# Moving two operands of TensorE to other places modulo 256 in SBUF

## The chip, the cores and the metric

The kernel runs on one core of one Trainium2 chip. The metric is the device time of one execution in microseconds. Before the change, three runs took 605.35, 607.12 and 607.37 us; their median is 607.12. One further execution was profiled.

## What the reference computes

Attention in which each query sees the keys of a narrow window and a summary of every block of 32 keys (the maximum of the keys, the mean of the values), and then a feed-forward layer with a squared ReLU:

```python
# q, k, v: (4, 8, 768, 64); block 32, window 16
k_sum = k.reshape(B, H, nb, block, D).max(axis=3)
v_sum = v.reshape(B, H, nb, block, D).mean(axis=3)
scores_l = scale * np.matmul(q, k.transpose(0, 1, 3, 2))     # kept where |i - j| < window
scores_s = scale * np.einsum('bhsd,bhnd->bhsn', q, k_sum) + np.log(block)
a = softmax(concatenate([scores_l masked, scores_s]))
x = np.matmul(a, concatenate([v, v_sum]))                     # -> (3072, 512)
h = x @ w_in                                                  # w_in (512, 2048)
g = s * np.maximum(h, 0.0) ** 2 + b
out = g @ w_out                                               # w_out (2048, 512)
```

## The kernel before, in words

The 3072 tokens are worked off in 12 chunks `c` of 256. The order of all work is written out by hand in one long string of step names (`FIRST_ORDER`, `REST_ORDER`); each engine takes its own instructions in that order, and all transfers are issued from SyncE's queue. Each operand of the large matrix products is split in two float32r parts, an upper one (`xh`, `wh`, `gh`) and a lower one (`xl`, `wl`, `gl`), and a product is three matmuls: lower by upper, upper by lower, upper by upper.

For a chunk, the steps are:
- scores `S` (L307), masks and exponentials, turned blocks on VectorE (L388), values `V` (L439); these give the attended rows `xh` and `xl`.
- the hidden layer `H` (L507): for each of 16 slices `f` of 128 hidden units, 12 matmuls of 256 columns into `ph`. The moving operand is `xh` or `xl`, the stationary one (loaded into the array ahead of the matmul) a slice of `wl` or `wh`. Two slices, 24 matmuls, share one bank `ph`.
- for each pair `q` of slices: ScalarE takes ReLU and square out of `ph` into a tile `g`, GpSimd applies `s` and `b` and forms sums of g's parts (L573 to L582), ScalarE rounds them into the upper half of a tile `gs` (L589), VectorE subtracts that for the lower half (L593).
- the output layer. Chunks 0 to 3 do it as `P` (L552), 6 matmuls of 512 columns a slice. Chunks 4 to 11 do it as `p` (`project_seven`, L672): for each `q`, seven products of sums instead of eight, 21 matmuls of 256 columns into four banks `acc`. The stationary operand is a part of `gs`. The moving one is a weight (`wh`, `wl`, 12 matmuls) or a sum of weights (9 matmuls), which is streamed from HBM into the tile `ring`.

In the steady part the order on TensorE is H of two slices (24 matmuls), p of one `q` (21), and so on; once a chunk, H of four slices (48), the values and scores of the next chunks, and p of two `q` (42) follow each other. In chunk 11 and the end of chunk 10 no scores are left to do.

The sums of weights are made once, in the tile `spare` (the same place as `ring`, earlier in time), and stored in HBM as `combos`. For chunks 4 to 11, `load_combo` (L612) loads three parts of 128 x 512 float32 for each `q` into one half of `ring`. The last two `q` of chunk 11 use tiles `late` instead: four lie in the places of the values (`vw`), two in a place of `qk`.

Places in SBUF come from the pools in the order in which they are opened; within a pool, tiles follow each other, each padded to 32 bytes. In bytes of a partition, the program before has these places:

| tile | pool | start | start modulo 256 |
|---|---|---|---|
| `wh` (and other slots) | slots | 4352 + 8192 n | 0 |
| `wl` | wring | 69888 + 4096 n | 0 |
| `ring`, `spare` | arena | 135424 | 0 |
| `kraw`, `vraw`, `o` | stage | 147712, 151808 | 0 |
| `ksum`, `rs` | small | 155904 and on | several |
| `gs` (both halves) | acts | 157120, 164288 | 192 |
| `r`, `g` | acts | 171456, 175552 | 192 |
| `xh`, `xl`, `pT` and others | p2 | 179648 and on | 192 for the large ones |
| `qk` | p3 | 207360, 213280 | 0, 32 |
| `vw` (and four `late`) | p3 | 219200 + 2048 n | 64 |

The parts of these tiles that TensorE reads start at multiples of 512 bytes (stationary) or 1024 bytes (moving) behind the tile's start, so modulo 256 they lie where the tile lies. The lower half of `gs` starts 3584 = 14 x 256 bytes behind the upper.

Of the kernel before, what the change touches and what calls it, by code (L numbers as in the profile page):

```python
# [9 lines left out]
F32 = mybir.dt.float32  # L10
# [7 lines left out]
P = 128  # L18
# [26 lines left out]
def windowed_attention_then_relu2_ffn(ctx, tc, qk, vwin, kt, vt, kq, vrow, wp, out):  # L45
# [4 lines left out]
    const = ctx.enter_context(tc.tile_pool(name="const", bufs=1))  # L50
    slots = ctx.enter_context(tc.tile_pool(name="slots", bufs=NF // 2))
    wring = ctx.enter_context(tc.tile_pool(name="wring", bufs=NF))
    arena = ctx.enter_context(tc.tile_pool(name="arena", bufs=1))
    stage = ctx.enter_context(tc.tile_pool(name="stage", bufs=2))
    kept = ctx.enter_context(tc.tile_pool(name="kept", bufs=1, space=bass.MemoryType.DRAM))
    small = ctx.enter_context(tc.tile_pool(name="small", bufs=2))
    acts = ctx.enter_context(tc.tile_pool(name="acts", bufs=2))
    p2 = ctx.enter_context(tc.tile_pool(name="p2", bufs=2))
    p3 = ctx.enter_context(tc.tile_pool(name="p3", bufs=3))
    ps_po = ctx.enter_context(tc.tile_pool(name="ps_po", bufs=2, space=bass.MemoryType.PSUM))  # L60
# [918 lines left out]
```

## Time and profile before

| | |
|---|---|
| median of three runs | 607.12 us |
| the profiled execution | 605.87 us |
| its span, first to last instruction | 603.9 us |
| granted TensorE clock, mean | 0.995 |
| TensorE busy | 584.5 us (97%) |
| VectorE busy | 438.2 us (73%) |
| ScalarE busy | 349.0 us (58%) |
| GpSimd busy | 299.5 us (50%) |
| DMA traffic | 127.34 MB, 211 GB/s on average |

A share of busy time is an average over stages. In views that group instructions a row has the line in the kernel, the engine and operation, what is written and read, how often it ran, the busy time in us and the mean length of one in ns. A matmul's length includes its way through the array, so matmuls overlap: the pace is read from the starts, or from the length of a whole piece divided by its count. The chain of work that ended last is followed back from the last instruction; in order of time it lists pieces with their start and length. PE is TensorE's matmul, PEld its loading of the stationary operand, DVE VectorE, ACT ScalarE, POOL GpSimd, SP SyncE.

### The profile page before, as it was taken

To read this page: it belongs to the slowest core of one execution; us is meant where nothing else is said; L and a number is where in the kernel's file an instruction comes from. 1 tells how busy PE (TensorE), PEld (TensorE's weight loads), DVE (VectorE), ACT (ScalarE), POOL (GpSimd) and SP (SyncE) were. 2 spreads that over 40 slices of the span, in tenths; PEclk is the share of its full clock that TensorE was granted. 3 is DMA by queue.
4 is the path that set the end of the run, shared out by engine and by line. 5 is a ranking of instruction groups with operands and counts; after the bars stand their busy time and mean duration, and the time that the engine had idled before them with its cause. 6 is when DMAs were issued, how large, how long until landed. Compare 5 with 4: busy or idle time off the path is not lost.

```text
span 603.9 us, 15345 instructions
## 1 busy us (share of the span) xinstructions
PE 584.5 (97%) x5816; PEld 555.0 (92%) x5816; DVE 438.2 (73%) x1033; ACT 349.0 (58%) x808; POOL 299.5 (50%) x499
## 2 busy tenths in 40 slices
PE   6999999999999998889999999999999999999996
PEld 5798898889899897889999999999999999999996
DVE  6999988799698699675698689587588488322323
ACT  5999899275596662733563564563563563433432
POOL 5320012590584563356645655655745755635643
PEclk9999999999999999899999999999999999999999
DMA  8999633064634974877776886765766756564540
GB/s 349 384 394 381 240 116 114 1 210 124 223 108 145 345 234 147 277 245 241 249 240 195 256 257 186 257 188 196 242 181 197 239 180 186 173 221 150 178 149 35
DMA packets 65401, 127.34 MB, mean 211 GB/s; under 512 B 7408, under 2 KB 17648, under 8 KB 65328
## 3 DMA queue, kind: packets, MB, share of 16 engines
q1 hardware_dynamic: 65328, 126.38, 62.9%
q8 instruction: 45, 0.74, 0.5%
q14 instruction: 28, 0.23, 0.1%
HBM read 111.52 MB, written 14.68 MB: 209 GB/s over the span
## 4 chain that ended last, share of the span: by engine, by line
PE 70%; DVE 12%; ACT 7%; DMA 6%; issue 2%; SPq 1%; POOL 1%; DVEq 0%; ACTq 0%; POOLq 0%
PE ph L507 33%; PE acc L672 24%; PE po L552 6%; DVE pT L388 4%; PE pav L439 3%; PE ps L307 2%; DMA qk<-in_qk_dram 2%; DMA ring<-combos 2%; DVE gs L539 1%; ACT wraw L124 1%; ACT wraw L123 1%; DVE qk L330 1%; DVE vhalf L173 1%; DMA wraw<-in_wp_dram 1%; DVE spare L642 1%
## 5 line engine op out<-in xcount | busy, mean ns | idle before, releaser
L593 DVE TENSOR_TENSOR gs<-g,gs 128x896 fp32r<-128x896 f32 x64 | 70.8, 1106 | 102.0 <-ACT gs L589 101.3
L565 ACT ACTIVATE g<-ph 128x512 f32<-128x512 f32 x64 | 38.3, 598 | 161.4 <-PE ph L507 138.7
L573 POOL TENSOR_SCALAR g<-g,sb_col 128x512 f32<-128x512 f32 x64 | 64.2, 1003 | 132.7 <-ACT g L569 116.6
L388 DVE STREAM_TRANSPOSE pT<-qk 32x256 f32<-32x256 f32 x288 | 125.6, 436 | 4.8
L672 PE MATMUL acc<-wh,gs 128*128 128x256 f32 x512 | 121.2, 280 | 0.2 <-DVE gs L593 0.2
L507 PE MATMUL ph<-xh,wl 128*128 128x256 f32 x760 | 120.0, 280 | 0.4 <-DVE wl L145 0.4
L507 PE MATMUL ph<-xh,wh 128*128 128x256 f32 x760 | 118.7, 278 | 0.0
L507 PE MATMUL ph<-xl,wh 128*128 128x256 f32 x760 | 118.6, 278 | 0.0
L507 PEld LDWEIGHTS ph<-xh,wl 128*128 128x128 f32 x760 | 103.9, 189 | 4.6 <-ACT r L521 1.2
L507 PEld LDWEIGHTS ph<-xl,wh 128*128 128x128 f32 x760 | 101.7, 188 | 0.0
L507 PEld LDWEIGHTS ph<-xh,wh 128*128 128x128 f32 x760 | 101.4, 188 | 0.0
L672 PE MATMUL acc<-ring,gs 128*128 128x256 f32 x558 | 95.2, 279 | 3.4 <-DMA ring<-combos 3.4
L672 PEld LDWEIGHTS acc<-wh,gs 128*128 128x128 f32 x512 | 91.6, 188 | 1.5 <-issue 0.8
L672 PEld LDWEIGHTS acc<-ring,gs 128*128 128x128 f32 x558 | 78.1, 188 | 4.0 <-DMA ring<-combos 4.0
L552 PE MATMUL po<-wh,gs 128*128 128x512 f32 x224 | 76.7, 394 | 0.0
L672 PE MATMUL acc<-wl,gs 128*128 128x256 f32 x256 | 71.2, 278 | 0.0
L589 ACT CAST gs<-g 128x896 fp32r<-128x896 f32 x64 | 59.9, 936 | 17.3 <-PE acc L672 9.3
L269 POOL COPY vw<-vsum 24x256 f32<-24x256 f32 x88 | 40.9, 498 | 46.1 <-DMA vw<-in_vwin_dram 19.6
L349 ACT ACTIVATE qk<-qk,mn 128x120 f32<-128x120 f32 x144 | 55.1, 384 | 5.6 <-DVE mn L330 4.9
L552 PE MATMUL po<-wl,gs 128*128 128x512 f32 x128 | 50.2, 392 | 0.0
L552 PEld LDWEIGHTS po<-wh,gs 128*128 128x128 f32 x224 | 42.1, 188 | 8.4 <-DVE mn L330 0.2
L578 POOL TENSOR_TENSOR g<-g 128x256 f32<-128x256 f32 x64 | 47.0, 734 | 4.6
(134 smaller groups left out, 918.4 us busy)
## 6 DMA issues: line engine op xcount, KB each, us to landing
ring<-combos SPq DMA_DIRECT2D x186, 256.0 KB
wraw<-in_wp_dram SPq DMA_DIRECT2D x32, 512.0 KB
qk<-in_qk_dram SPq DMA_DIRECT2D x44, 369.0 KB
vw<-in_vwin_dram SPq DMA_DIRECT2D x48, 256.0 KB
combos<-spare SPq DMA_DIRECT2D x16, 512.0 KB
out_dram<-o SPq DMA_DIRECT2D x24, 256.0 KB
kraw<-in_kt_dram SPq DMA_DIRECT2D x12, 384.0 KB
vraw<-in_vt_dram SPq DMA_DIRECT2D x12, 252.0 KB
```

The lines of the kernel that those rows point to most:

```text
L269: nc.gpsimd.tensor_copy(vw_t[c, p][WIN:KR, e], vsum[bi][WIN : WIN + NB, 2 * p + e, :].unsqueeze(1).to_broadcast([NB, NSUB, D]),)
L349: nc.scalar.activation(pr, pr, AF.Exp, bias=mn_of[c, p][:, n : n + 1], scale=-1.0, accum_out=sums_of(c, p)[:, n : n + 1])
L388: nc.vector.transpose(to[BLOCK * k : BLOCK * (k + 1), :, rows], src)
L439: nc.tensor.matmul(oi, vw[:KR, e, i, :], pi[:KR], start=True, stop=True)
L507: nc.tensor.matmul(ph, w[:, kc * P : (kc + 1) * P], x[:, kc], start=(n == 0), stop=(n == len(terms) - 1))
L552: nc.tensor.matmul(po[c, t], a[:, t * P : (t + 1) * P], w[:, 512:], start=(f == 0 and n == 0), stop=(f == NF - 1 and n == len(terms) - 1),)
L565: nc.scalar.activation(gg[c, q][:, : 2 * T], ph_of.pop((c, q)), AF.Relu)
L573: nc.gpsimd.tensor_scalar(g, g, s_col, b_col, ALU.mult, ALU.add)
L578: nc.gpsimd.tensor_tensor(g[:, 4:6], g[:, 0:1].to_broadcast([P, 2, P]), g[:, 1:3], ALU.subtract)
L589: nc.scalar.copy(halves[c, q][0], gg[c, q][:, P:])
L593: nc.vector.tensor_tensor(gl, gg.pop((c, q))[:, P:], gh.bitcast(F32), ALU.subtract)
L672: nc.tensor.matmul(to, g[:, k], w, start=(q == 0 and side == 0 and m == 0), stop=(q == NF // 2 - 1 and m == 2 and side == (bank != "m")),)
```

## The change

Three pools are opened, each with one tile that nothing writes or reads: 64 bytes a partition ahead of `arena`, 128 bytes ahead of `acts` and 64 bytes ahead of `p2`.

```diff
     wring = ctx.enter_context(tc.tile_pool(name="wring", bufs=NF))
+    ctx.enter_context(tc.tile_pool(name="gap_arena", bufs=1)).tile([P, 16], F32, name="gap_arena")
     arena = ctx.enter_context(tc.tile_pool(name="arena", bufs=1))
     stage = ctx.enter_context(tc.tile_pool(name="stage", bufs=2))
     kept = ctx.enter_context(tc.tile_pool(name="kept", bufs=1, space=bass.MemoryType.DRAM))
     small = ctx.enter_context(tc.tile_pool(name="small", bufs=2))
+    ctx.enter_context(tc.tile_pool(name="gap_acts", bufs=1)).tile([P, 32], F32, name="gap_acts")
     acts = ctx.enter_context(tc.tile_pool(name="acts", bufs=2))
+    ctx.enter_context(tc.tile_pool(name="gap_p2", bufs=1)).tile([P, 16], F32, name="gap_p2")
     p2 = ctx.enter_context(tc.tile_pool(name="p2", bufs=2))
```

By the order of the pools, what lies behind the first gap starts 64 bytes later: `ring` and `spare` at 64 modulo 256, and with them `stage` and `small`, also by 64. What lies behind the second starts 192 bytes later: `gs`, `r` and `g` at 128 modulo 256. Behind the third, all is 256 bytes later, so `p2` and `p3` keep their places modulo 256. The order of the instructions, their shapes, their waits and the transfers are the same.

## The prediction

> **What bounds the kernel now.** I began with the page of the profiled execution: busy shares, then the chain that ended last.
>
> ```profile
> span 603.9 us, 15345 instructions
> PE 584.5 (97%) x5816; PEld 555.0 (92%) x5816; DVE 438.2 (73%) x1033; ACT 349.0 (58%) x808; POOL 299.5 (50%) x499
> ...
> PE ph L507 33%; PE acc L672 24%; PE po L552 6%; DVE pT L388 4%; PE pav L439 3%; PE ps L307 2%; DMA qk<-in_qk_dram 2%; DMA ring<-combos 2%; DVE gs L539 1%; ACT wraw L124 1%; ACT wraw L123 1%; DVE qk L330 1%; DVE vhalf L173 1%; DMA wraw<-in_wp_dram 1%; DVE spare L642 1%
> ```
>
> TensorE is busy 97% of the span, and the chain lies on its matmuls of L507 (the hidden layer, H) and L672 (the seven products, p). So what the change is worth is decided by the pace of these matmuls, and by whether any operand comes late. The next view is the chain in order of time, in one chunk of the steady part; the columns are start, length in us, and what.
>
> ```profile
> 395.31 2.83 PE ph L507 x24
> 398.14 2.47 PE acc L672 x21
> 400.61 2.73 PE ph L507 x24
> 403.35 2.38 PE acc L672 x21
> 405.73 2.83 PE ph L507 x24
> ...
> 416.15 2.83 PE ph L507 x24
> ...
> 424.18 2.38 PE acc L672 x21
> 426.57 5.65 PE ph L507 x48
> 432.22 2.01 PE pav L439 x64
> ...
> 436.04 5.02 PE acc L672 x41
> ```
>
> The chain has no holes. But TensorE has two paces for the same work. 24 matmuls of H take 2.73 or 2.83 us, which is 113.8 or 117.9 ns each; 21 of p take 2.38 or 2.47, 113.3 or 117.6 ns. The paces alternate: slow H, slow p, quick H, quick p, slow H. So a pace survives the step from H to p, and changes at the step from p to H. A matmul at the slow pace costs 4.1 to 4.3 ns more; I use 4.2.
>
> Which data are read does not explain it. In H the moving operand is x (192 modulo 256) and the stationary one a weight (0); in p the moving one is a weight or the ring (0) and the stationary one a half of g (192). Both paces occur with both. The last two chunks show that the product's number does not explain it either:
>
> ```profile
> 525.97 5.14 PE acc L672 x42
> 531.11 2.73 PE ph L507 x24
> ...
> 562.37 5.46 PE ph L507 x48
> 567.83 4.76 PE acc L672 x42
> 572.59 2.83 PE ph L507 x24
> ```
>
> The 42 products that start a chunk are slow at 525.97 (122 ns each, their restart included) and quick at 567.83 (113.3), on the same buffers; at 531.11 the same step from p to H made H quick, where the one behind 436.04 is followed by a slow H in the other chunks. So the pace has a memory, and a step from p to H usually tips it.
>
> **The change, part by part.** It adds three empty tiles of 64, 128 and 64 bytes a partition. No instruction, wait, queue entry or byte of traffic is added, so the fixed part of the sum is 0. What moves, by the order of the pools: the ring tile (and `spare`, the same place earlier) from 0 to 64; behind it also `stage` and `small`, by 64; all of `acts`, g and its halves alike, from 192 to 128; `p2` by 256, so its places modulo 256 stay, and `p3` likewise. Five things could cost.
>
> (1) The landing of the ring, 186 loads of 2048 bytes a partition. The trace has loads of the same packet size to both kinds of place: values go to 64 modulo 256 (390.5 to 391.5, where values alone are under way), ring parts to 0 (575.0 to 576.0, ring alone). From the DMA view of both windows:
>
> ```profile
> DMA packets 192, 0.36 MB, mean 361 GB/s; under 512 B 23, under 2 KB 23, under 8 KB 191
> ...
> q1 hardware_dynamic: 191, 0.34, 89.5%
> ...
> DMA packets 160, 0.28 MB, mean 279 GB/s; under 512 B 24, under 2 KB 24, under 8 KB 160
> ...
> q1 hardware_dynamic: 160, 0.28, 72.7%
> ```
>
> Values: 0.895 x 16 engines x 1.0 us = 14.3 us over 168 large packets (191 less 23 small ones), 85 ns; ring: 0.727 x 16 = 11.6 us over 136, 86 ns. So nothing, with 2 ns as a generous bound (the small packets are counted into both). A ring load is 8 packets on each of 16 engines, so 16 ns late at most, on loads for which TensorE waited 3.4 us three times in all (quoted below). I take 0; bound 0 to 0.05 us.
>
> [...]
>
> (2) VectorE, ScalarE and GpSimd on g and its halves, all now at 128 where all were at 192, so their offsets to one another stay.
>
> ```profile
> L593 DVE TENSOR_TENSOR gs<-g,gs 128x896 fp32r<-128x896 f32 x64 | 70.8, 1106 | 102.0 <-ACT gs L589 101.3
> L573 POOL TENSOR_SCALAR g<-g,sb_col 128x512 f32<-128x512 f32 x64 | 64.2, 1003 | 132.7 <-ACT g L569 116.6
> ...
> L349 ACT ACTIVATE qk<-qk,mn 128x120 f32<-128x120 f32 x144 | 55.1, 384 | 5.6 <-DVE mn L330 4.9
> ...
> L349 ACT ACTIVATE spare<-spare,mn 128x120 f32<-128x120 f32 x32 | 12.3, 388 | 0.1
> ...
> PE acc L672 <- DMA ring<-combos: 3.4, 3, 2.4
> ...
> PE acc L672 <- DVE gs L593: 0.2, 1, 0.2
> ```
>
> The same exponential at two differently placed tiles takes 384 and 388 ns: 1% either way is the bound, 11 ns on the 1106. VectorE stands idle 102 us ahead of this subtraction, and TensorE waited 0.2 us for its result in the whole run. If that cover were gone, 64 x 11 ns = 0.7 us would show, as later p groups. I take 0.
>
> (3) `stage` and `small`, 64 further: the row loads, the output rows and their stores. Priced as (1) and (2), off TensorE's path but for the last store: 0.
>
> (4) TensorE's reading inside p. Moving and stationary operand now lie 64 apart (weights 0 against halves 192). Afterwards the ring against the halves is 64 to 128, again 64 apart, but weights against halves is 0 to 128: apart by 128. The trace has that distance in one place only: `late`, at 64 in the four `vw` places, against halves at 192. The `late` parts at 0 follow it.
>
> ```profile
> L672 PE MATMUL acc<-ring,gs 128*128 128x256 f32 x558 | 95.2, 279 | 3.4 <-DMA ring<-combos 3.4
> L672 PE MATMUL acc<-late,gs 128*128 128x256 f32 x18 | 3.1, 281 | 0.0
> ...
> 594.66 0.52 PE L672 MATMUL acc<-late,gs 128*128 128x256 f32 x3
> 595.01 0.28 PE L672 MATMUL acc<-wh,gs 128*128 128x256 f32 x1
> ...
> 597.14 0.52 PE L672 MATMUL acc<-late,gs 128*128 128x256 f32 x3
> 597.50 0.28 PE L672 MATMUL acc<-wh,gs 128*128 128x256 f32 x1
> ```
>
> From three `late` matmuls at 64 to the next matmul it is 0.35 us, from three at 0 it is 0.36: no difference at this resolution. The mean lengths, 281 against 279 ns, bound it at 2 ns. It would meet 12 of the 21 matmuls of each p, 768 in eight chunks, and 384 of 512 columns in the four chunks before (L552), where the halves also stand against weights: 1152 x 2 ns = 2.3 us. I take 0.2 us, near the timeline's nothing. No row excludes a gain; rival B prices that.
>
> (5) TensorE's reading at the steps between H and p. Now operands of neighbouring matmuls coincide modulo 256 there: from H to p, x and the halves both at 192; from p to H, ring and weight both at 0. Afterwards both pairs stand 64 apart, as inside H today. The steps from p to H are where the pace tips, so this part touches the seat of the two paces. I cost it at 0 for the forecast because the two chunk starts above show different outcomes on the same places: something other than the place carries the pace, and the instruction order, which the change leaves alone, is the nearest candidate. Its bounds are the rivals.
>
> [...]
>
> Sum: 0 + 0 + 0 + 0.2 + 0 = 0.2 us on the execution's own 605.87 us (603.9 of span, 2.0 around it), 606.1. The median of the runs, 607.12, is 1.25 above that execution; I forecast on its scale, 607.3 us.
>
> **The rivals.** A chunk of 360 matmuls has, by the rows above, 3 x 45 + 48 + 42 = 225 slow and 135 quick ones. Sums of L672 (512 + 558 + 256 + 18 = 1344, 168 a chunk) make eight chunks.
>
> B, *the tipping ends on the quick side* (faster). If coinciding places are what throws the pace from quick to slow, taking them away keeps a quick pace quick. All quick: 8 x 225 x 4.2 ns = 7.6 us less, 599.5. More likely some restarts still begin slow, as at 525.97: about half, 603.5. For it: the tipping sits at exactly the steps whose distance changes, and in the middle chunks H behind L552 (weight against weight, again 0 on 0) also begins slow:
>
> ```profile
> 180.16 0.64 PE L507 MATMUL ph<-xh,wl 128*128 128x256 f32 x4
> 180.64 0.62 PE L507 MATMUL ph<-xl,wh 128*128 128x256 f32 x4
> 181.09 0.62 PE L507 MATMUL ph<-xh,wh 128*128 128x256 f32 x4
> ```
>
> The first four take 0.48 us, the next four 0.45. Against it: from H to p operands coincide as well, and nothing tips.
>
> C, *the pace sticks on the slow side* (slower). The same steps also throw slow back to quick, four times a chunk. Each chunk's products start slow behind the values and scores (436.04). If no step tips, that pace lasts the whole chunk. Price: 8 x 135 x 4.2 ns = 4.5 us, 611.8 with the forecast's 0.2. It decides where a chunk's first H behind the double group is slow and the next one is slow too; up to two quick pairs left a chunk it is still 2 us, slower. Against it: what L552 does, where H recovers by itself in the fifth matmul.
>
> D, *the change does not do what it says*: the places do not come out as listed, or no reader feels them; 607.1.
>
> **How the numbers follow.** Forecast 0.40, B 0.32, C 0.24, D 0.04. A measurement of this kernel tells about 0.3% (1.8 us) from no change; its own three runs lie 2.0 us apart. So faster is B's share, same is the forecast and D less what falls out of the band, slower is C and that rest: 0.32, 0.42, 0.26. The forecast's own range is 605.5 to 609.5 (run scatter, and 2.3 us of part 4). Into B the range goes to 602.0, past its half, leaving out about 0.13; into C to 611.5, just short of all slow, leaving out 0.06.
>
> **What would show it.** In the chain in order of time, the pieces of 24 and 21 must keep alternating between 2.83/2.47 and 2.73/2.38: then part 5 is right. All pieces at 2.73/2.38 show B, all at 2.83/2.47 C. The mean length of L672 on `wh` against `ring` shows part 4; waits of TensorE for `ring` and `gs` over 4 us would break parts 1 and 2. A third pace, below 113 or above 118 ns, in p alone would make the prediction wrong in a way that no rival prices.

## The result, and the profile after

The changed kernel took 610.45 us, the median of 9 runs (608.84 to 614.23), where the kernel before took 607.12 in the same comparison (605.35 to 608.1). The two medians lie 3.3 us apart. The ratio on record is 1.0083, with a 95% interval from 1.0063 to 1.0104, which would be 3.8 to 6.3 us; it is not the quotient of the two medians, which is 1.0055. By either figure the kernel is slower, and all nine runs after lie above all nine before. The forecast was no change, 607.3.

The page of the profiled execution after, which took 612.74 us: busy shares and three of the costliest groups (busy us, mean ns of one, idle time before them).

```profile
span 611.0 us, 15345 instructions
PE 593.2 (97%) x5816; PEld 563.3 (92%) x5816; DVE 438.3 (72%) x1033; ACT 349.4 (57%) x808; POOL 300.3 (49%) x499
...
L675 PE MATMUL acc<-wh,gs 128*128 128x256 f32 x512 | 123.9, 285 | 0.2 <-DVE gs L596 0.2
...
L675 PE MATMUL acc<-ring,gs 128*128 128x256 f32 x558 | 96.8, 282 | 4.0 <-DMA ring<-combos 4.0
...
L596 DVE TENSOR_TENSOR gs<-g,gs 128x896 fp32r<-128x896 f32 x64 | 71.2, 1113 | 109.1 <-ACT gs L592 108.5
```

and, of the kernel before, the row on `wh`:

```profile
L672 PE MATMUL acc<-wh,gs 128*128 128x256 f32 x512 | 121.2, 280 | 0.2 <-DVE gs L593 0.2
```

The instructions are the same 15345; the lines stand three further down (H is L510, p is L675). TensorE is busy 8.7 us longer, and the other engines hardly: VectorE 438.3 against 438.2 us, its subtraction 1113 ns against 1106. The products grew by 3 ns on the ring (279 to 282) and 5 ns on `wh` (280 to 285).

The same kernel's waits of TensorE (in all, times, longest):

```profile
PE acc L675 <- DMA ring<-combos: 4.0, 3, 2.4
...
PE acc L675 <- DVE gs L596: 0.2, 1, 0.2
```

They were 3.4 and 0.2 us. The 0.6 us more on the ring belong to the first products of chunk 4: TensorE reached them 0.79 us sooner than before (247.47 us against 248.26) and waited there for the same loads. So no wait explains the loss. What did change is seen in the chain in order of time (start, us, what):

```profile
260.99 2.59 PE acc L675 x15
263.59 3.77 PE ph L510 x24
...
393.74 5.13 PE acc L675 x42
398.87 2.83 PE ph L510 x24
401.70 2.50 PE acc L675 x21
404.20 2.83 PE ph L510 x24
...
430.83 5.65 PE ph L510 x48
...
440.30 5.13 PE acc L675 x42
```

and, for the length of a chunk, two rows of the same view of the kernel before:

```profile
390.17 5.14 PE acc L672 x42
...
436.04 5.14 PE acc L672 x42
```

The alternation of 2.83/2.47 and 2.73/2.38 is gone. From chunk 5 on every 24 matmuls of H take 2.83 us (117.9 ns each) and every 21 of p 2.50 (119.0 on average). From one double group (p of two `q`, 42 matmuls) to the next it is 46.56 us (440.30 - 393.74) where it was 45.87 (436.04 - 390.17): 0.69 us a chunk. The pieces say where it comes from: three H of a chunk go from 2.73 to 2.83 (0.30), three p from 2.38 to 2.50 (0.36), three p from 2.47 to 2.50 (0.09), together 0.75 by rounded lengths.

That this is pace, with no waiting and no clock in it, shows in the windows over the same four chunks (stretch, length, TensorE busy and matmuls recorded, granted clock, DMA share, GB/s); of the kernel before:

```profile
298.44:481.90 183.46, 183.46 (x1953) 1.00 0.70 221
```

and of the kernel after, with one stretch of chunk 4 ahead of it:

```profile
262.00:266.00 4.00, 4.00 (x23) 0.57 0.85 242
...
300.62:486.86 186.24, 186.24 (x1953) 1.00 0.69 218
```

TensorE is busy without a gap in both, at a granted clock of 1.00, and the four chunks take 2.78 us more. The 7.1 us between the two spans thus split up: 2.18 up to the first of these double groups (298.44 and 300.62), 2.78 in these four chunks, 1.62 in the next two, 0.52 at the end. Of the first 2.18, 1.5 us comes with a lower granted clock around 262 us (0.57 over these 4 us, where the kernel before had 1.00): 15 products took 2.59 us where the same 15 took 2.03 before, and 24 of H 3.77 where the later ones take 2.83. That is no part of the change: the run e3 below, whose pace is that of before, takes 2.82 and 3.54 us for the same two pieces. So 5.6 us of the 7.1 is the change in this pair of executions, more than the 3.3 us between the medians and inside the interval of the ratio.

### The profile page after: what moved, and what is told of

Read it like the earlier page. It is cut to its first block, busy times and chain, and to the rows that moved or that the text cites. A ratio compares the mean times of both kernels' runs of the same rounds, so it can differ in the third digit from the quotient of the medians.

```text
span 611.0 us, 15345 instructions
## 1 busy us (share of the span) xinstructions
PE 593.2 (97%) x5816; PEld 563.3 (92%) x5816; DVE 438.3 (72%) x1033; ACT 349.4 (57%) x808; POOL 300.3 (49%) x499
## 4 chain that ended last, share of the span: by engine, by line
PE 65%; DVE 14%; ACT 8%; DMA 6%; issue 3%; SPq 2%; POOL 1%; DVEq 0%; ACTq 0%; POOLq 0%
PE ph L510 31%; PE acc L675 25%; DVE pT L391 5%; PE po L555 4%; PE pav L442 3%; DMA ring<-combos 2%; PE ps L310 2%; DMA vraw<-in_vt_dram 2%; DVE gs L542 1%; ACT wraw L126 1%; DVE spare L645 1%; ACT wraw L127 1%; DVE vhalf L176 1%; ACT pr L352 1%; DMA qk<-in_qk_dram 1%
## 5 line engine op out<-in xcount | busy, mean ns | idle before, releaser
L596 DVE TENSOR_TENSOR gs<-g,gs 128x896 fp32r<-128x896 f32 x64 | 71.2, 1113 | 109.1 <-ACT gs L592 108.5
L675 PE MATMUL acc<-wh,gs 128*128 128x256 f32 x512 | 123.9, 285 | 0.2 <-DVE gs L596 0.2
L510 PE MATMUL ph<-xh,wl 128*128 128x256 f32 x760 | 120.9, 281 | 0.1
L510 PE MATMUL ph<-xl,wh 128*128 128x256 f32 x760 | 120.2, 281 | 0.0
L510 PE MATMUL ph<-xh,wh 128*128 128x256 f32 x760 | 120.1, 280 | 0.0
L510 PEld LDWEIGHTS ph<-xh,wl 128*128 128x128 f32 x760 | 105.2, 190 | 4.0 <-DVE wl L148 0.8
L510 PEld LDWEIGHTS ph<-xh,wh 128*128 128x128 f32 x760 | 102.7, 189 | 0.0
L510 PEld LDWEIGHTS ph<-xl,wh 128*128 128x128 f32 x760 | 102.7, 189 | 0.0
L675 PE MATMUL acc<-ring,gs 128*128 128x256 f32 x558 | 96.8, 282 | 4.0 <-DMA ring<-combos 4.0
L675 PEld LDWEIGHTS acc<-wh,gs 128*128 128x128 f32 x512 | 92.4, 189 | 1.4 <-issue 0.8
L675 PEld LDWEIGHTS acc<-ring,gs 128*128 128x128 f32 x558 | 79.5, 189 | 4.8 <-DMA ring<-combos 4.6
L675 PE MATMUL acc<-wl,gs 128*128 128x256 f32 x256 | 72.1, 282 | 0.0
```

The source lines that it names most:

```text
L510: nc.tensor.matmul(ph, w[:, kc * P : (kc + 1) * P], x[:, kc], start=(n == 0), stop=(n == len(terms) - 1))
L596: nc.vector.tensor_tensor(gl, gg.pop((c, q))[:, P:], gh.bitcast(F32), ALU.subtract)
L675: nc.tensor.matmul(to, g[:, k], w, start=(q == 0 and side == 0 and m == 0), stop=(q == NF // 2 - 1 and m == 2 and side == (bank != "m")),)
```

## The experiments

The two paces of TensorE are called quick (113.3 to 113.8 ns a matmul of 256 columns) and slow (117.6 to 118). My theory after the result was that the places of the operands relative to one another, modulo 256, decide at the step from p to H whether the pace tips, and that this is one effect of ring and halves together. The rivals were that one moved operand alone is read more slowly where it now lies, that the absolute place counts, and that one of the other tiles moved along (`stage`, `small`) does it.

This table has all runs; each ratio goes against runs of the kernel before in the same comparison (medians of 605.25 to 607.12 us), and the chunk is read, as above, between the double groups around 390 and 436 us.

| kernel | ring / halves | H | p | chunk, us | us | ratio (95%) |
|---|---|---|---|---|---|---|
| before | 0 / 192 | alternates | alternates | 45.87 | 607.12 | |
| after | 64 / 128 | all slow | all slow, 119.0 | 46.56 | 610.45 | 1.0083 (1.0063 to 1.0104) |
| e1_ring_only | 64 / 192 | all quick | 116.2 | 45.46 | 602.53 | 0.9941 (0.9916 to 0.9966) |
| e2_halves_only | 0 / 128 | slow behind the double group, then quick | 119.0 | 45.98 | 606.82 | 1.0010 (0.9984 to 1.0036) |
| e3_others_only | 0 / 192 | as before | as before | 45.87 | 606.61 | 1.0011 (0.9987 to 1.0035) |
| e4_halves_at_64 | 0 / 64 | quick but for one piece | slow | 45.70 | 604.61 | 0.9973 (0.9951 to 0.9996) |
| e5_ring_128 | 128 / 192 | all slow | all slow | 46.41 | 611.09 | 1.0087 (1.0055 to 1.0119) |
| e6_ring_128_halves_64 | 128 / 64 | all quick | 118.1 | 45.65 | 604.60 | 0.9976 (0.9951 to 1.0001) |
| e7_lower_weights_128 | 0 / 192, `wl` at 128 | quick, 114.8 | slow, 118.1 | 45.84 | 605.79 | 1.0005 (0.9981 to 1.0030) |
| e8_all_by_64 | 64 / 0, weights 64, x 0 | as before | as before | 45.86 | 605.32 | 1.0006 (0.9973 to 1.0040) |
| e9_one_tip | 128 / 192 | one quick a chunk, else slow | 116.2 once, else slow | 46.30 | 609.81 | 1.0067 (1.0043 to 1.0091) |
| e10_last_part_64 | 0, 0, 64 / 192 | alternates or all slow | alternates or all slow | 45.66; 46.46 when slow | 607.40 | 1.0029 (1.0010 to 1.0048) |
| e11_last_part_back | 64, 64, 0 / 128 | all quick | slow | 45.70 | 604.30 | 0.9983 (0.9961 to 1.0005) |
| e12_last_part_192 | 0, 0, 192 / 192 | alternates | alternates | 45.76 | 606.13 | 1.0012 (0.9981 to 1.0043) |

In all of them the weights lie at 0 and x at 192 unless the table says otherwise, and every kernel issues the same instructions; only e9 issues two groups of them in another order. The edits are empty tiles in pools of their own, in this form, with 16 (64 bytes), 32 or 48 floats:

```diff
+    ctx.enter_context(tc.tile_pool(name="gap_arena", bufs=1)).tile([P, 16], F32, name="gap_arena")
```

### The three parts of the change, each alone

**e1_ring_only**: the ring at 64, all else as before.

```diff
+ gap of 64 bytes ahead of arena, gap of 192 bytes ahead of stage
```

> Only the ring is moved to 64 modulo 256; stage, small, g, its halves and all behind keep their places modulo 256. Theory T1 (the step from p to H tips the pace because the last moving operand, the ring, and the weight loaded meanwhile lie at the same place modulo 256): that coincidence is gone, so the pace sticks on the slow side as in the changed kernel, pieces of 24 at 2.83 us throughout, about 611 us. Theory T2 (weights and halves 128 apart inside p are what slows): weights against halves are 64 apart as before, so the alternation of 2.83 and 2.73 stays, 607 to 608 us.

It took 602.53 us, 0.9941 of the kernel before. The chain in order of time:

```profile
387.76 5.15 PE acc L674 x42
...
423.96 5.45 PE ph L509 x48
...
433.22 5.15 PE acc L674 x42
438.37 2.73 PE ph L509 x24
441.10 2.44 PE acc L674 x21
```

Every H is quick, the one behind the double group too, and p takes 2.44 us, between 2.38 and 2.47. A chunk is 45.46 us. So the first half of the change, by itself, is a gain: rival B of the prediction, which was priced at 603.5 with half of the slow pieces made quick. T1 and T2 both missed it. The timeline of one p shows why its 2.44 us lie between the two paces:

```profile
400.65 0.28 PE L674 MATMUL acc<-wh,gs 128*128 128x256 f32 x1
...
401.33 0.51 PE L674 MATMUL acc<-ring,gs 128*128 128x256 f32 x3
...
403.10 0.62 PE L509 MATMUL ph<-xh,wl 128*128 128x256 f32 x4
```

The six matmuls ahead of the ring take 0.68 us (113 ns each), the fifteen from there on 1.77 (118). So this p starts quick and is slow from its first matmuls on the ring, which now lie 128 from the halves: the pace can turn inside a group too.

**e2_halves_only**: g and its halves at 128, all else as before.

```diff
+ gap of 192 bytes ahead of acts, gap of 64 bytes ahead of p2
```

> Only g and its halves are moved, to 128 modulo 256; the ring stays at 0, the rest keeps its places modulo 256. T1: ring and weight still coincide at the step from p to H, so the pace goes on tipping, pieces of 24 alternate, 607 to 608 us, and p itself may run at a third pace near 119 ns. T2: weights against halves are 128 apart, all pieces slow, about 611 us. A third possibility is that the step from H to p (x and halves, both at 192 before, now 64 apart) is needed for the tipping: then all slow as well, with p at 2.50.

It took 606.82 us, ratio 1.0010. Its chain:

```profile
397.21 2.82 PE ph L509 x24
400.04 2.50 PE acc L674 x21
402.53 2.74 PE ph L509 x24
...
438.01 5.18 PE acc L674 x42
443.19 2.82 PE ph L509 x24
```

Here only the H behind the double group is slow, and the others are quick, a gain; p takes 2.50 us throughout, as in the changed kernel, a loss; the two nearly cancel. The time and p's pace are those that T1 expected, the pieces of H are not: the alternation is gone although ring and weight still coincide. Neither part alone slows the kernel. A sum of the two, -0.6% and +0.1%, would be -0.5%; together they give +0.8%. So the loss is not that either operand is simply read more slowly at its new place.

**e3_others_only**: `stage` and `small` 64 further on, ring, g and halves where they were modulo 256 (256 bytes further on).

```diff
+ gap of 64 bytes ahead of stage, gap of 192 bytes ahead of acts
```

> Only stage and small are moved by 64; ring, halves, x and weights keep their places modulo 256 (all behind stage stands 256 bytes further on). T1 and T2: nothing that TensorE reads in H or p changes modulo 256, so the time stays at 607 us with the alternation of 2.83 and 2.73. If stage and small, or places beyond 256 bytes, were the cause, it would be 610 us or more.

It took 606.61 us, ratio 1.0011, and its pieces alternate as before, with the same 45.87 us a chunk. So `stage` and `small` do not cause the loss, and 256 bytes more for halves and x change nothing.

### Other distances

**e4_halves_at_64**: halves at 64, ring at 0. **e5_ring_128**: ring at 128, halves at 192. **e6_ring_128_halves_64**: both. **e7_lower_weights_128**: the lower weights `wl` at 128, all else as before. **e8_all_by_64**: everything that TensorE reads in H and p 64 further on, so that each distance is that of before.

```diff
  e4
+ gap of 128 bytes ahead of acts, gap of 128 bytes ahead of p2
  e5
+ gap of 128 bytes ahead of arena, gap of 128 bytes ahead of stage
  e6
+ gap of 128 bytes ahead of each of arena, stage, acts and p2
  e7
+ gap of 128 bytes ahead of wring, gap of 128 bytes ahead of arena
  e8
+ gap of 64 bytes ahead of slots
```

> g and its halves at 64 modulo 256, ring at 0: weights and ring against halves are 64 apart the other way round (the halves ahead), x against halves 128 apart, ring against weight coincide. T1: the step from p to H still tips, alternation, 607 us. T2: weights and halves are 64 apart, so no slowing by 128, alternation, 607 us. If the step from H to p needs its coincidence, all slow at 611 us, or all quick near 600 us if that step is what throws the pace to slow.

e4 took 604.61 us, ratio 0.9973: from chunk 5 on H is quick (2.74 us for 24) but for the first piece behind the double group of chunk 10 (531.62, 2.83), and p slow (2.47 for 21). None of the expectations has this pattern.

> Only the ring is moved, to 128 modulo 256; halves and x stay at 192, weights at 0. Theory T3 (what counts is the distance modulo 256 between the matmul's moving operand and the stationary operand loaded meanwhile: 64 or 192 inside a group allows two lasting paces, quick 113.3 ns and slow 117.8 ns; 128 inside a group forces a slow one near 119 ns; the distance at the step between groups decides which one follows): inside p all distances are 64 or 192 again, so p can be quick where it was slow with the ring at 64. The step from p to H is now 128. If that step leaves the pace alone, and H enters quick, all is quick: pieces of 24 at 2.73 and of 21 at 2.38, about 599 us. If it tips as a distance of 0 does, the alternation stays, 606 us. A theory that only the ring at exactly 64 is good gives 606 us or more.

e5 took 611.09 us, ratio 1.0087, as slow as the changed kernel, with the halves where they were. Its chain:

```profile
393.35 5.14 PE acc L674 x42
398.49 2.83 PE ph L509 x24
401.32 2.47 PE acc L674 x21
403.79 2.83 PE ph L509 x24
...
439.76 5.14 PE acc L674 x42
```

All slow, at 46.41 us a chunk. So the loss of the changed kernel is not tied to its own places: another pair gives it too. T3 expected 599 or 606 us and missed.

> Ring at 128, g and halves at 64, x at 192, weights at 0. T3: inside p the distances are 192 (weights) and 64 (ring), so two paces are possible; from H to p the distance is 128, which threw p to slow in the run with halves alone at 64, so H quick at 2.73 and p slow at 2.47, 603 to 605 us. If the ring at 128 keeps p quick, 599 to 601 us.

e6 took 604.60 us, ratio 0.9976. The ring at 128, which made e5 slow in every piece, is here beside halves at 64, and H is all quick (2.73), as T3 expected: again it is the pair that counts.

> Only the lower weights (wl) are moved, to 128 modulo 256; ring at 0, halves and x at 192, upper weights at 0. T3: H begins with wl as its stationary operand, so the step from p to H is 128 instead of 0, inside H and p all distances stay 64 or 192. If a distance of 0 at that step is what tips, the tipping ends although the ring has not moved: one pace throughout, all quick 599 us or all slow 611 us. If the tipping stays, the coincidence at this step is not its cause, 606 us.

e7 took 605.79 us, ratio 1.0005: H almost quick (2.75 or 2.76 us), p slow (2.48). Moving a third operand also breaks the alternation, but H and p do not get one pace throughout, which T3 expected where the tipping ends.

> Everything from the upper weights on is moved by 64, so all distances between weights, ring, halves and x stay as before while every place modulo 256 changes. T3 (distances alone count): same alternation of 2.83 and 2.73, same 606 us. A theory of absolute places (64 is bad for the ring, 128 for the halves) gives another pattern or time.

e8 took 605.32 us, ratio 1.0006. Its chain:

```profile
394.89 2.83 PE ph L508 x24
397.71 2.47 PE acc L673 x21
400.19 2.73 PE ph L508 x24
402.92 2.38 PE acc L673 x21
```

This is the kernel before, piece by piece. All four kinds of operands have moved by 64 modulo 256 and nothing has changed. So the absolute place does not count, as far as this one shift shows (45.86 us a chunk against 45.87); the distances do.

### Where the pace is handed over

**e9_one_tip**: e5, with the last two products of `q` = 1 exchanged in chunks 4 to 10, so that the double group ends on a weight (0) and not on the ring (128), once a chunk. All places stay those of e5.

```diff
  e5, and in do():
+        if name[0] == "p" and name[1:].split(".")[1:] in (["1", "5"], ["1", "6"]) and name[1:].split(".")[0] != "11":
+            name = name[:-1] + {"5": "6", "6": "5"}[name[-1]]
```

> Ring at 128 as in the run where every piece was slow, and for q = 1 of chunks 4 to 10 the last two of the seven products change places, so that this p ends on a weight (at 0, the weight loaded meanwhile at 0): the step that tips in the kernel before, now once a chunk, right behind the slow double group. Places are the same as in that all-slow run but for nothing. T3 with memory (the step from a ring at 128 leaves the pace as it is, quick or slow): from the first H behind the double group on all is quick, 24 at 2.73 and 21 at 2.38, until the next scores, about 600 us. If a ring at 128 makes slow of itself, H or p turns slow again at the first p that ends on the ring, 608 to 611 us.

It took 609.81 us, ratio 1.0067. Its chain:

```profile
436.08 5.14 PE acc L674 x42
441.22 2.74 PE ph L509 x24
443.96 2.44 PE acc L674 x21
446.40 2.83 PE ph L509 x24
```

In chunks 5 to 10 the H right behind the exchanged products is quick, at the one place of the chunk that was touched; only the first six matmuls of the p behind it are quick (0.68 us), and from its products on the ring on all is slow. That is the second of the two expectations; the 600 us of T3 were missed. In chunk 4, where the products had just waited for the ring, the H behind them stays slow (2.83 at 261.23). So what p ends on has a hand in the pace of H, though not alone. Other engines' reads and writes lie where they lie in e5, so this speaks for TensorE's own operands. It is worth 0.11 us a chunk (46.41 to 46.30), too little for the two ratios to tell apart.

**e11_last_part_back**: the changed kernel, with only the last third of each half of the ring, which the last product reads, put back to 0 modulo 256.

```diff
  the changed kernel, and
-            held["ring"] = arena.tile([P, 3072], F32R, name="ring", tag="ring")
+            held["ring"] = arena.tile([P, 3200], F32R, name="ring", tag="ring")
-        k = 512 * (3 * (q % 2) + n)
+        k = 1600 * (q % 2) + 512 * n + 48 * (n == 2)
```

> The changed kernel, with only the third of the ring that the last product of each p reads taken back to 0 modulo 256; the other two thirds stay at 64, g and its halves at 128. T3 (the last product and its step alone hand the pace to H): the last moving operand and the weights coincide again and are 128 from the halves, as with the halves alone moved, so H turns quick, 24 at 2.73 behind nearly every p, while p stays slow near 2.50: 606 to 608 us. If H is slow in the changed kernel because of what p as a whole is, H stays at 2.83 and the time at 610 us.

It took 604.30 us, ratio 0.9983 to the kernel before. Its chain:

```profile
388.19 5.15 PE acc L675 x42
...
424.62 5.46 PE ph L510 x48
...
433.89 5.15 PE acc L675 x42
439.04 2.74 PE ph L510 x24
441.77 2.48 PE acc L675 x21
```

Every H is quick (24 in 2.74, 48 in 5.46 us), as T3 expected, and a chunk takes 45.70 us where the changed kernel took 46.56; the time is lower than the 606 to 608 us that were expected. Three of the 21 matmuls of a p read from another place, and the 24 of H behind them change their pace. This is the strongest reading of the study: the loss in H sits at the last product of p and the step from it to H.

**e10_last_part_64** and **e12_last_part_192**: the kernel before, with the last third of each half of the ring at 64 or at 192.

```diff
  e10 and e12, the tile as in e11; e10:
+        k = 1600 * (q % 2) + 512 * n + 16 * (n == 2)
  e12:
+        k = 1600 * (q % 2) + 512 * n + 48 * (n == 2)
```

> The kernel before, with only the third of the ring that the last product of each p reads moved by 64 (places 64 modulo 256); weights, the other two thirds, halves and x as before. T3: 18 of 21 products are 64 from the halves as before and can be quick, the last three are 128 away; the step from p to H is then the one that made H quick each time in the run with the whole ring at 64. So 24 at 2.73 throughout, 21 near 2.40, about 599 us, faster than both kernels. If the three products at 128 bring back a slow p, 602 to 603 us as there; if the tipping has another seat, the alternation, 606 us.

e10 took 607.40 us, ratio 1.0029. In e1 a last product at 64 went with an H that was always quick; here it does not. Its chain, in chunks 5, 7 and 10:

```profile
303.48 2.83 PE ph L507 x24
306.31 2.48 PE acc L672 x21
308.79 2.83 PE ph L507 x24
...
395.59 2.73 PE ph L507 x24
398.32 2.39 PE acc L672 x21
400.71 2.83 PE ph L507 x24
...
530.75 2.83 PE ph L507 x24
```

The same program, on the same places, runs chunks 5 and 10 all slow and chunks 6 to 9 alternating. So the last product's place is not the whole of it: the earlier products of p, or the pace that was there before, count too. The slow chunks use up what the others gain: chunks 5 to 10 take 269.92 us (298.33 to 568.25) where the kernel before took 269.39 (298.44 to 567.83). The medians lie 1.8 us apart (607.40 against 605.63); whether other executions have more slow chunks, the one profiled cannot show. The 599 us of T3 were missed.

> The kernel before, with only the third of the ring that the last product of each p reads moved to 192 modulo 256, where the halves lie too (distance 0 in the last three matmuls, 192 at the step to H). So far a p that was quick until its last product has always been followed by a slow H (distances 64, 128 or 192 there), and a slow p was followed by a quick or a slow one. If the distance at the step decides alone, 192 keeps the pace inside H and would leave a quick p followed by a quick H: all quick, 599 us, or all slow, 611 us. If a quick p is followed by a slow H whatever the place, H and p alternate as before, 605 to 608 us.

e12 took 606.13 us, ratio 1.0012, alternating as before with the order turned: in chunks 5 to 9 the H behind the double group is quick (2.72) and the next slow (2.83). That is the last of the three expectations: a quick p is again followed by a slow H. No layout tried beats e1.

## Why the prediction was wrong

The measured 610.45 us lies beyond the forecast's own 605.5 to 609.5, and inside the wider range only because that was stretched toward rival C.

**Steps (1), (2) and (3), at 0, were right.** A packet of 2048 bytes took 84 ns before and after (median, 570 to 590 us, where most land in the ring), TensorE waited 4.0 us for the ring and 0.2 for the halves, VectorE's subtraction stayed within the 1% bound (1113 against 1106 ns), and e3 shows 1.0011 for `stage` and `small`.

**Step (4), p with weights and halves 128 apart, was too small.** I took 0.2 us from a timeline of six matmuls. A slow p of 21 went from 2.47 to 2.50 us, which over 6 pieces in each of 8 chunks is 1.4 us, inside the bound of 2.3. It is the third pace above 118 ns that the prediction named as a sign that no rival prices. The 128 alone does not make it: e11 has the same distance between weights and halves, and its p takes 2.47 or 2.48. In the first four chunks, where the halves also stand 128 from the weights, twelve matmuls of 512 columns went from 2.75 us (169.20 to 171.95 in the timeline of before) to 2.78 (169.19 to 171.97), some 2.5 ns each, 0.9 us over 352 of them. It does not show in the time: the first products of chunk 4 began at 247.47 us where they had begun at 248.26, and waited there for the ring as before.

**Step (5), the steps between H and p, at 0, failed, and with it the sign.** I had put the seat of the paces at the step from p to H, which e9 and e11 bear out for the pace of H, and then priced the change of that very step at nothing, "because the two chunk starts above show different outcomes on the same places: something other than the place carries the pace, and the instruction order, which the change leaves alone, is the nearest candidate". The inference was wrong. Two outcomes on the same places show that the place alone doesn't determine the pace; they don't show that it has no part in it. With one and the same order of instructions, the runs have H alternating (before), all quick (e1, e6, e11) and all slow (after, e5). Together with the third pace of p, what stood at 0 is 5.6 us in the traces.

**Rival C is what happened**, but for the third pace of p: no step tips any more, and the pace sticks on the slow side, from the H behind the double group on (398.87, then 404.20), as C's condition had it. Its price was 4.5 us and 611.8; with the 1.4 us of p it is 5.9, against 5.6 in the traces and 3.3 between the medians. (With two quick pairs left a chunk, C's price would be 8 x 45 x 4.2 ns = 1.5 us, not the 2 us that stand there.) What I held against C, that H behind L552 recovers by itself (0.48 us for its first four matmuls, 0.45 for the next), came from a step of other operands, weight on weight, and didn't carry over. Rival B is as real: it is what the ring alone does (602.53). Both lay in the tipping, and I found no row of the kernel before that tells which of the two a new distance would bring.

**What the distances are between.** e8 against e1 and e5 shows that the places of TensorE's operands count relative to one another: 605.32 us with all of them moved together, 602.53 and 611.09 with the ring alone. TensorE loads while it multiplies: in the kernel after, matmuls are busy for 593.2 us and loads for 563.3 of a span of 611.0, so both for at least 545.5. That what counts is what TensorE streams against what it loads meanwhile is my reading; no run isolates it.

**Open.** What in the chip holds the pace was not found, nor why p is slower still (119.0) in the changed kernel and in e2, and not in e11. Slow in every piece were only the two layouts whose last product has the ring 192 ahead of the halves (64 - 128 and 128 - 192, modulo 256) while the next weight is not at the ring's own place; e4 has the first without the second and e6 the second without the first, and in both H is quick. That fits the layouts with a whole ring at one place, but it was not tested by itself, and e10 shows that more than these two distances counts. Nor was a layout found in which H and p are both quick throughout.

## What to carry to other kernels

Where TensorE is the bound and each matmul loads a new stationary operand, read its pace piece by piece from the chain in order of time; two lengths for the same piece of work are a gain to look for, and the places of the operands modulo 256 are worth a run each, pair by pair, since two moves can each be harmless and cost 0.8% together. A seat that is found in the trace must be priced at its bounds when a change touches it: that the same places gave two outcomes is a reason for a wide range, not for a zero. Here the best of the layouts tried is the ring alone at 64, 0.9941 of the kernel before.

## What the runs showed of the hardware that was not expected

- At a granted clock of 1.00 the same matmul of 256 float32r columns with its load takes 113.3 or 117.9 ns, 4% apart, and kept that pace over groups of 21 to 48 matmuls (p of 21 in 2.38 or 2.47 us, H of 48 in 5.46 or 5.65). The pace turned where one group follows the other (before: p of 2.47, then H of 2.73), or inside a group (p in e1, from 113 to 118 ns); moving what three matmuls read changed the pace of the next 24 (e11: 2.74 us where the changed kernel took 2.83).
- Absolute places did not count, distances modulo 256 did: 64 bytes for all operands together, or 256 for halves and x, change nothing (e8, 45.86, and e3, 45.87 us a chunk, against 45.87), while 64 for the ring alone does (e1, 45.46).
- The places alone didn't decide the pace: within one execution, e10 runs chunks 5 and 10 all slow (24 of H in 2.83 us) and chunks 6 to 9 alternating (2.73 and 2.83), on the same places modulo 256.
